# Gated linear attention into a feed-forward layer on one core: blocks of three units become blocks of four, and the second product keeps the weights standing

## The chip, the core and the metric

The kernel runs on one core of a Trainium2 chip. The metric is the device time of one execution in microseconds; each figure for a kernel is a median over runs. TensorE multiplies, VectorE (DVE) and ScalarE (ACT) work elementwise, GpSimd (POOL) does the rest, SyncE (SP) issues the DMAs. Line numbers L... are lines of the kernel before, unless the text says after.

## The reference

Inputs are q, k, v and alpha of shape 4 x 8 x 768 x 48 (batch, heads, sequence, head size) and the weights w_in (384 x 2048) and w_out (2048 x 384). Only what matters:

```python
state = np.zeros((B, H, D, D))
for t in range(S):
    state = alpha[:, :, t, :, None] * state + np.einsum('bhd,bhe->bhde', k[:, :, t], v[:, :, t])
    y[:, :, t] = np.einsum('bhd,bhde->bhe', q[:, :, t], state)
x = y.transpose(0, 2, 1, 3).reshape(B * S, H * D)     # 3072 x 384
h = x @ w_in
g = np.maximum(0.01 * h, h)
out = g @ w_out                                        # 3072 x 384
```

The weights arrive as 64-bit floats, handed over as 64-bit integers, and the kernel turns them into pairs of 32-bit floats itself.

## The kernel before

**Attention.** The 768 positions are cut into 6 chunks of 128. A unit is one chunk of one batch with its 8 heads, so there are 24 units; unit u is chunk u // 4 of batch u % 4. For a unit the kernel builds running products of alpha by scans (`scans`, L282 to L300), scales q and k by them (L308 to L322), multiplies k by q into 128 x 128 scores per head (`scores`, L330), masks these (L333 to L346), turns k (`k_tokens`, L348), and forms y from the scores and the state (`outputs`, L358 to L392) and the new state (`next_state`). y is split into a high and a low part in fp32r (the format in which TensorE reads these floats at a faster rate), which are the input x of the FFN. `attention(first, last)` is a generator that yields between these steps; steps of unit u and u + 1 alternate in it. The first 9 units (`AHEAD`) load q, k and alpha by token, and TensorE transposes them (L258); later units load them in 32 x 4 pieces, four DMAs per tensor (L135), and VectorE turns them by stream transposes (L262).

**FFN.** Three units make a block (`UPB` 3): 384 tokens, 8 blocks. The inner size 2048 is cut into 16 slices f. For each block and slice, `ffn_in` multiplies three weight tiles by x into a 128 x 384 bank in three products each (high by high, high by low, low by high), nine matmuls of 384 columns (L460), ACT and VectorE apply the activation and split the result in `gh` and `gl` (L463 to L472). `ffn_out` (L477 to L489) multiplies it by w_out: the activations of one unit (128 tokens) stand in the array, 384 columns of the weights move, three products for each of three units, nine matmuls (L485). That is 8 x 16 x 18 = 2304 matmuls. A block's sums over f lie in three PSUM banks. `finish` copies each bank by ACT (L495) and writes it out by one DMA of 192 KB (L497), whose rows are 1536 bytes.

**Order.** The weights of a slice f come by six DMAs (L188, L192) and are converted by two ACT and six VectorE operations over 128 x 768 (`converting`, L205 to L243). The tile framework emits instructions in the order of the program, and moves them by its own simulated timeline; `behind` and `issue_after` fix an instruction behind another. The prologue runs the attention of units 0 to 8 and converts slices 0 to 2. Then the slices of blocks 0 and 1 alternate, f by f, with the conversion of the slices ahead of them; the second product follows the first `LAG` 3 items later. From block 2 on the attention of units 9 to 23 runs between the products: each item advances the generator by a set number of steps (`SL`, `LEAD`), some held back behind the `gl` of the last items of blocks 0 and 1 (`HELD`). The line that places them:

```python
items += [(i, f, (SL + (LEAD if i == 2 else 0)) / NF, "b") for i in range(2, NB) for f in range(NF)]
```

The x of a block lies in one of three slots of `large`; `gather` (L409) fills up the last rows by two DMAs. PSUM has two banks `ph` for the first product, three named a and three named b. While blocks 0 and 1 alternate, b holds the sums of block 0 and a those of block 1; later b holds the sums of a block, and a serves the attention.

## Time and profile before

| | |
|---|---|
| median of 3 runs | 540.48 us (540.3 to 542.23) |
| the profiled run | 540.7 us |
| its span, from the first to the last instruction | 539.0 us |
| TensorE busy | 520.6 us, 97% |
| VectorE busy | 380.3 us, 71% |
| ScalarE busy | 234.1 us, 43% |
| mean granted TensorE clock | 0.996 |

The trace is one execution. A window row has a stretch, its length, and for each engine the busy time and, in brackets, the number of instructions. A row of the chain of waits has the start in us, the length, and the engine, the tile and the line that the end of the program goes back to; "DMA" or "issue" in place of an engine is time in which a transfer or nothing visible is waited for; SPq is SyncE's own queue. In the groups a shape such as 128x384 is partitions by elements, and the number ahead of the vertical bar is how many instructions there are.

### The profile page before, as it was taken

The page shows a single profiled execution, that of the slowest core. Times are in us where ns is not written, and L with a number is a line of the kernel's source. Part 1 is how long each engine was busy: PE and PEld are TensorE (multiplying, and loading weights), DVE is VectorE, ACT ScalarE, POOL GpSimd, SP SyncE. Part 2 cuts the span into 40 slices and gives each one's busy share as a digit, 9 for nine tenths or more (in the row PEclk, how much of TensorE's full clock was granted, in tenths as well). Part 3 has the DMA queues.
Part 4 walks back from the last instruction along what each step waited for, and adds up shares of the span by engine and source line. Part 5 has one row for each costly group of instructions (what it writes and reads, how often), then busy time and mean ns, then how long its engine had stood idle before and what let it go on. Part 6 is the DMA issues. An engine that isn't in the chain of part 4 may idle for free.

```text
span 539.0 us, 9954 instructions
## 1 busy us (share of the span) xinstructions
PE 520.6 (97%) x3742; PEld 497.8 (92%) x3742; DVE 380.3 (71%) x694; ACT 234.1 (43%) x494; POOL 64.5 (12%) x140
## 2 busy tenths in 40 slices
PE   6998899999999899999999999999999999999996
PEld 4787789999998799999999999999999999999995
DVE  6899999999999597875685775775876533333331
ACT  2675665545532543435334343344343344233332
POOL 4445420000000022110110101001100000000000
PEclk9998999999999999999999999999999999999999
DMA  9999954545825343433332422413301010101001
GB/s 146 164 177 184 202 140 131 142 111 134 190 43 144 114 107 85 102 79 103 71 82 58 105 64 61 105 42 99 69 1 40 0 45 1 23 0 45 0 1 49
DMA packets 92981, 46.62 MB, mean 86 GB/s; under 512 B 57856, under 2 KB 90112, under 8 KB 92928
## 3 DMA queue, kind: packets, MB, share of 16 engines
q1 hardware_dynamic: 92928, 45.93, 39.4%
q8 instruction: 31, 0.51, 0.4%
q14 instruction: 22, 0.18, 0.1%
HBM read 38.83 MB, written 4.72 MB: 81 GB/s over the span
## 4 chain that ended last, share of the span: by engine, by line
PE 87%; DVE 5%; DMA 3%; issue 1%; SPq 1%; POOL 1%; ACT 1%; DVEq 0%; ACTq 0%; POOLq 0%
PE ph L460 35%; PE b L485 32%; PE a L330 4%; PE a L485 4%; PE a L374 3%; PE a L368 2%; PE b L258 2%; PE a L353 1%; DMA raw<-in_moe_w_in_dram 1%; DMA out_dram<-t 1%; PE a L385 1%; DVE pc L288 1%; PE b L374 1%; PE a L258 1%; DVE rc L294 1%
## 5 line engine op out<-in xcount | busy, mean ns | idle before, releaser
L460 PE MATMUL ph<-large,w 128*128 128x384 f32 x1152 | 225.6, 338 | 3.1 <-DMA raw<-in_moe_w_in_dram 1.9
L460 PEld LDWEIGHTS ph<-large,w 128*128 128x128 f32 x1152 | 200.5, 188 | 5.4 <-DVE t L466 2.2
L485 PE MATMUL b<-w,gh 128*128 128x384 f32 x672 | 169.6, 340 | 1.3 <-ACT t L495 1.3
L466 DVE TENSOR_TENSOR t<-ph,t 128x384 f32<-128x384 f32 x128 | 70.3, 549 | 86.7 <-ACT t L463 86.3
L485 PEld LDWEIGHTS b<-w,gh 128*128 128x128 f32 x672 | 119.5, 188 | 3.7 <-ACT t L495 1.6
L463 ACT ACTIVATE t<-ph 128x384 f32<-128x384 f32 x128 | 62.6, 489 | 136.7 <-PE ph L460 128.6
L468 ACT CAST gh<-t 128x384 fp32r<-128x384 f32 x128 | 65.7, 513 | 108.2 <-DVE t L466 104.7
L485 PE MATMUL b<-w,gl 128*128 128x384 f32 x336 | 107.3, 336 | 0.0
L472 DVE TENSOR_TENSOR gl<-t,gh 128x384 fp32r<-128x384 f32 x128 | 70.3, 550 | 33.6 <-ACT gh L468 30.0
L485 PEld LDWEIGHTS b<-w,gl 128*128 128x128 f32 x336 | 62.6, 188 | 0.1
L341 POOL TENSOR_SCALAR_AFFINE_SELECT sm<-sm 128x512 f32<-128x512 f32 x33 | 21.9, 676 | 117.6 <-ACT sm L340 100.0
L346 POOL TENSOR_TENSOR small<-us,pe 48x192 f32<-48x192 f32 x40 | 25.5, 637 | 85.2 <-DVE us L406 75.3
L330 PEld LDWEIGHTS a<-qs,ks 48*128 48x128 f32 x312 | 26.0, 191 | 6.5 <-issue 5.2
L330 PE MATMUL a<-qs,ks 48*128 48x128 f32 x312 | 31.0, 289 | 0.9 <-DVE ks L321 0.9
L298 POOL COPY pe<-pc 128x4 f32<-128x4 f32 x24 | 5.7, 240 | 175.3 <-DVE pc L288 175.2
L262 DVE STREAM_TRANSPOSE ks<-small 128x512 f32<-128x512 f32 x15 | 16.6, 1119 | 13.6 <-PE a L353 13.6
L340 ACT COPY sm<-a 128x512 f32<-128x512 f32 x24 | 14.0, 584 | 15.1 <-PE b L330 13.3
L288 DVE TENSOR_TENSOR_SCAN pc<-e,small 128x128 f32<-128x128 f32 x60 | 19.9, 391 | 0.0
L485 PE MATMUL a<-w,gh 128*128 128x384 f32 x96 | 19.5, 335 | 0.0
L294 DVE TENSOR_TENSOR_SCAN rc<-e,small 128x511 f32<-128x511 f32 x15 | 19.1, 1272 | 0.2
L374 PE MATMUL a<-sm,small 128*48 128x128 f32 x256 | 18.1, 277 | 1.1 <-POOL sm L341 1.1
L224 ACT ACTIVATE raw<-raw 128x768 f32<-128x768 f32 x16 | 14.6, 915 | 7.0 <-DMA raw<-in_moe_w_in_dram 7.0
(82 smaller groups left out, 542.5 us busy)
## 6 DMA issues: line engine op xcount, KB each, us to landing
raw<-in_moe_w_out_dram SPq DMA_DIRECT2D x16, 384.0 KB, 4.0
small<-in_v_dram SPq DMA_DIRECT2D x24, 192.0 KB, 3.9
raw<-in_moe_w_in_dram SPq DMA_DIRECT2D x32, 144.0 KB, 4.0
out_dram<-t SPq DMA_DIRECT2D x24, 192.0 KB, 2.0
small<-in_alpha_dram SPq DMA_DIRECT2D x32, 96.0 KB, 2.2
small<-in_q_dram SPq DMA_DIRECT2D x30, 96.0 KB, 2.5
small<-in_k_dram SPq DMA_DIRECT2D x30, 96.0 KB, 2.2
small<-in_alpha_dram SPq DMA_DIRECT2D x30, 80.0 KB, 2.4
```

The source lines that it names most:

```text
L288: nc.vector.tensor_tensor_scan(pc[:, p, :], aT[:, p, :], ones.broadcast_to([P, C]), 1.0, ALU.mult, ALU.mult)
L294: nc.vector.tensor_tensor_scan(flat[2][:, NP * C - 2::-1], flat[0][:, NP * C - 1:0:-1], flat[1][:, NP * C - 2::-1], last, ALU.mult, ALU.add)
L330: nc.tensor.matmul(ss[s][:, p, :], ks[lo:lo + D, p, :], qs[lo:lo + D, p, :], start=True, stop=True)
L341: nc.gpsimd.affine_select(out=sm[s], in_=sm[s], compare_op=ALU.is_ge, fill=0.0, base=0, pattern=[[0, NP], [1, C]], channel_multiplier=-1)
L346: nc.gpsimd.tensor_tensor(*scalings.pop(0))
L374: nc.tensor.matmul(y[lo:lo + m, p, :], V[:, c:c + m], masked[u][s][:, p, :], start=not tb and p == 0, stop=p == NP - 1, skip_group_check=True,
L460: nc.tensor.matmul(ph, w_in_of(f, wn, g), xt[:, g, :], start=n == 0, stop=n == 3 * NG - 1)
L463: put(ordered, "ACT", lambda: nc.scalar.mul(t, ph, 0.01))
L466: put(ordered, "DVE", lambda: nc.vector.tensor_tensor(t, ph, t, ALU.max))
L468: put(ordered, "ACT", lambda: nc.scalar.copy(gh, t))
L472: made["gl", i, f] = put(ordered, "DVE", lambda: nc.vector.tensor_tensor(gl, t, gh.bitcast(F32), ALU.subtract))
L485: nc.tensor.matmul(po[j], gt[:, js], w_out_of(f, wn), start=f == 0 and n == 0, stop=f == NF - 1 and n == 2)
```

## The change

- `UPB` goes from 3 to 4 units: 6 blocks of 512 tokens, one chunk of all four batches each. `ffn_in` moves 512 columns in each of its nine matmuls (864 in all), and a bank `ph` is full.
- In blocks 0 to 4 (`TURNED`), `ffn_out` has the weights standing (three tiles of 128 output columns) and 512 columns of activations moving, in the order gh by high, gl by high, gh by low: 9 matmuls of 512 per slice, 720 in all, and three banks hold the sums with output columns as rows. The last block computes as before, with four banks and 12 matmuls of 384 per slice, 192 in all.
- `finish` of a turned block turns each bank by one stream transpose of VectorE (128x512, in 32 x 32 squares; after's line 526) into a tile `o` (three of them) and writes it out by 16 DMAs of 16 KB, 32x4x32 elements in pieces of 128 bytes: 48 DMAs per block (after's line 531).
- `AHEAD` is 8 units; units 10 and 11 too are transposed by TensorE (`on_pe`). `LAG` is 2. Block 0 runs two slices ahead of block 1 (`FORE`). Units 8 to 11 begin in the last slices of blocks 0 and 1, and the rest of them follows behind these; block 2 begins when they are done, and units 12 to 23 run between the products of blocks 2 to 5.
- x has two slots that share the part that is gathered from; the first products and transposes of the program get dummy matmuls beside them (`keep_warm`); the order of the four places of y in its bank turns with the block.

The diff, cut to what is named here and in the prediction:

```diff
--- before.py
+++ after.py
@@ -31,7 +31,7 @@
     NP = H // 2
     NG = DM // P
     NF = DF // P
-    UPB = 3
+    UPB = B
     HB = 64
     BR = HB + D
     GAP = HB - D
@@ -55,11 +55,16 @@
     T4 = 4
     RUN = T4 * D
     PITCH = RUN + GAP
-    AHEAD = 3 * UPB
-    LAG = 3
-    SOON, EARLY = 2, 3
-    LEAD = 8
+    AHEAD = 2 * UPB
+    FORE = 2
+    LAG = 2
+    LEAD, HELD = 9, 10
     SL = 8 * UPB
+    def on_pe(u):
+        return u < AHEAD or u in (AHEAD + 2, AHEAD + 3)
     kinds = ["a", "b"]
@@ -122,7 +127,7 @@
         tb, b = units[u]
         ts = slice(tb * C, (tb + 1) * C)
         t, src = loaded(u, i), (alpha, q, k)[i]
-        if u < AHEAD:
+        if on_pe(u):
             n = H if u or i else H // 2
             for h in range(0, H, n):
                 nc.sync.dma_start(
@@ -334,7 +352,7 @@
         ss = live[u].pop()
         sm = [atp.tile([P, NP, C], F32, name="sm", bufs=3) for _ in (0, 1)]
         for s in (0, 1):
-            if s and u >= AHEAD:
+            if s and not on_pe(u):
                 nc.vector.tensor_tensor(sm[s], ss[s], mask.unsqueeze(1).broadcast_to([P, NP, C]), ALU.mult)
                 continue
             made["sm", u] = nc.scalar.copy(sm[s], ss[s])
@@ -464,52 +483,79 @@
         for step in first:
             next(step, None)
         put(ordered, "DVE", lambda: nc.vector.tensor_tensor(t, ph, t, ALU.max))
-        gh = ffp.tile([P, TB], F32R, name="gh", bufs=LAG + 1)
+        gh, gl = (ffp.tile([P, TB], F32R, name=name, bufs=LAG + 1) for name in ("gh", "gl"))
         put(ordered, "ACT", lambda: nc.scalar.copy(gh, t))
         for step in second:
             next(step, None)
-        gl = ffp.tile([P, TB], F32R, name="gl", bufs=LAG + 1)
         made["gl", i, f] = put(ordered, "DVE", lambda: nc.vector.tensor_tensor(gl, t, gh.bitcast(F32), ALU.subtract))
         return gh, gl
     pos = {}
-    def ffn_out(i, f, gs, tag):
+    TURNED = NB - 1
+    NO = 3
+    def ffn_out(i, f, gs):
         gh, gl = gs
+        turned = i < TURNED
         if f == 0:
-            pos[i] = [bank(tag)[:, 0:DM] for _ in range(UPB)]
-        po = pos[i]
-        for j in range(UPB):
-            js = slice(j * C, (j + 1) * C)
-            for n, (gt, wn) in enumerate(((gh, HIGH), (gh, LOW), (gl, HIGH))):
+            tags = "bbb" if i == 0 else "aaa" if turned else "aaab"
+            pos[i] = [bank(tag)[:, 0:TB if turned else DM] for tag in tags]
+        for j, po in enumerate(pos[i]):
+            js = slice(j * P, (j + 1) * P)
+            for n, (gt, wn) in enumerate(((gh, HIGH), (gl, HIGH), (gh, LOW)) if turned else ((gh, HIGH), (gh, LOW), (gl, HIGH))):
+                w = w_out_of(f, wn)
                 nc.tensor.matmul(
-                    po[j], gt[:, js], w_out_of(f, wn), start=f == 0 and n == 0, stop=f == NF - 1 and n == 2
+                    po, *((w[:, js], gt) if turned else (gt[:, js], w)),
+                    start=f == 0 and n == 0, stop=f == NF - 1 and n == 2,
                 )
         if f == NF - 1:
             finish(i)
     def finish(i):
         for j, po in enumerate(pos.pop(i)):
-            tb, b = units[i * UPB + j]
-            o = ffp.tile([P, DM], F32, name="t")
-            nc.scalar.copy(o, po)
-            r = b * S + tb * C
-            nc.sync.dma_start(out[r:r + P, :], o)
-    items = []
-    for f in range(NF):
-        items += [(0, f, 0, "b"), (1, f, 0, "a")]
-    items += [(i, f, (SL + (LEAD if i == 2 else 0)) / NF, "b") for i in range(2, NB) for f in range(NF)]
-    gs = {}
-    LOADS = [(("v", 4), 0, 0), (("v", 5), 0, 1), (("v", 6), 1, 0), (("v", 7), 1, 1), (("g", 1), 2, None), (("g", 1), 3, None)]
-    STARTS = {62: ("kt", 7), 65: ("kv", 7)}
+            if i == TURNED:
+                tb, b = units[i * UPB + j]
+                o = (ffp.tile([P, TB], F32, name="o", bufs=NO) if j < NO else ffp.tile([P, TB], F32, name="t"))[:, 0:DM]
+                (nc.vector.tensor_copy if j % 2 else nc.scalar.copy)(o, po)
+                nc.sync.dma_start(out[b * S + tb * C:b * S + (tb + 1) * C, :], o)
+                continue
+            t = ffp.tile([P, TB], F32, name="o", bufs=NO)
+            nc.vector.transpose(t, po)
+            for a in range(4):
+                c = j * P + 32 * a
+                for b in range(B):
+                    r = b * S + i * C
+                    nc.sync.dma_start(
+                        out[r:r + C, c:c + 32].rearrange("(m r) c -> r m c", r=32),
+                        t[32 * a:32 * (a + 1)].rearrange("r (b m c) -> r b m c", b=B, c=32)[:, b],
+                    )
+    LOADS = [(("v", 4), 0, 0), (("v", 5), 0, 1), (("v", 6), 1, 0), (("v", 7), 1, 1), (("v", 7), 2, None), (("v", 7), 3, None)]
+    CONVERT = [5, 7]
+    STARTS = {50: ("kv", 5), 62: ("kt", 7)}
+    pending = []
+    def put_in(i, f, steps=None):
+        pending.append((i, f, ffn_in(i, f, steps)))
+    def put_out(n=0):
+        ffn_out(*pending.pop(n))
+    loaded_f = converted = 0
+    def load_next():
+        nonlocal loaded_f
+        if loaded_f < NF:
+            load_weights(loaded_f)
+            loaded_f += 1
     st = attention(0, AHEAD)
-    loaded_f = converted = 0
     for n, _ in enumerate(st):
         if n == 2:
             load_values(NV - 1)
@@ -518,61 +564,79 @@
             with behind(*key):
                 load_weights(f, part)
             loaded_f = f + 1
-        u = AHEAD - EARLY + converted
-        if converted < EARLY and ("ks", u) in made:
-            with behind("ks", u):
+        if CONVERT and ("ks", CONVERT[0]) in made:
+            u = CONVERT.pop(0)
+            with behind("ks", u), behind("sm", u - 1):
                 convert(converted)
             converted += 1
         if n in STARTS:
-            i, f = items[len(gs)][:2]
             with behind(*STARTS[n]):
-                gs[len(gs)] = ffn_in(i, f)
-    kinds[:] = "a"
-    HELD = [(0, 14), (1, 14), (0, 15)] + [(1, 15)] * 5
-    due, emitted = 0.0, 0
-    new = coming = None
-    for n in range(len(items) + LAG):
-        slices = 0
-        if n < len(items):
-            i, f, slices, _ = items[n]
-            if f == 0:
-                if i == 2:
-                    st, held = attention(AHEAD, NU), HELD
-                while i not in ready:
-                    next(st)
-                emitted, due = 0, 0.0
-            if loaded_f < NF:
-                load_weights(loaded_f)
-                loaded_f += 1
-                if loaded_f == NF:
-                    asked, later = later, None
-                    with behind("raw", NF - 1):
-                        for fn, *args in asked:
-                            fn(*args)
-            if n < len(STARTS):
-                pass
-            elif i == 0:
-                if coming is None:
-                    coming = converting(f + SOON, True)
-                    next(coming)
-                old, new, coming = new or iter(()), coming, converting(f + SOON + 1, True)
-                gs[n] = ffn_in(i, f, ((), (coming, new, old, new)))
-            elif i == 1:
-                gs[n] = ffn_in(i, f, ((new, new), (new,)))
-                next(new, None)
-            else:
-                gs[n] = ffn_in(i, f)
-        for half in range(2):
-            due += slices / 2
-            while emitted < due:
-                with behind("gl", *held.pop(0)) if held else nullcontext():
-                    next(st, None)
-                emitted += 1
-            if half == 0 and n >= LAG:
-                i, f, _, tag = items[n - LAG]
-                ffn_out(i, f, gs.pop(n - LAG), tag)
+                put_in(0, len(pending))
+    assert converted == len(pending) == FORE and not LOADS
+    with behind("x", AHEAD - 1):
+        for _ in converting(FORE, True):
+            pass
+    for _ in range(FORE + 1):
+        load_next()
+    st = attention(AHEAD, AHEAD + UPB)
+    new, coming = None, converting(FORE + 1, True)
+    next(coming)
+    put_out()
+    for f in range(NF - FORE):
+        new, coming = coming, converting(f + FORE + 2, True)
+        put_in(1, f, ((), (new, new, coming)))
+        put_out()
+        for _ in range(3):
+            next(new, None)
+        put_in(0, f + FORE, ((), (new,)))
+        next(new, None)
+        if f:
+            put_out()
+        load_next()
+        if loaded_f == NF and later is not None:
+            asked, later = later, None
+            with behind("raw", NF - 1):
+                for fn, *args in asked:
+                    fn(*args)
+        if f >= NF - FORE - 4:
+            with behind("gl", 0, f + FORE):
+                next(st)
+    kinds[:] = "b"
+    put_in(1, NF - 2)
+    put_out()
+    put_out()
+    put_in(1, NF - 1)
+    while pending:
+        for _ in range(8):
+            next(st)
+        put_out()
+    while 2 not in ready:
+        next(st)
+    st, held = attention(AHEAD + UPB, NU), HELD
+    for i in range(2, NB):
+        due, emitted = 0.0, 0
+        while i not in ready:
+            next(st)
+        for f in range(NF):
+            put_in(i, f)
+            for half in range(2):
+                due += (SL + (LEAD if i == 2 else 0)) / NF / 2
+                while emitted < due:
+                    with (behind("gl", i, f - 1) if f else behind("x", (i + 1) * UPB - 1)) if held else nullcontext():
+                        next(st, None)
+                    held = max(held - 1, 0)
+                    emitted += 1
+                if half == 0 and len(pending) > LAG:
+                    put_out()
+    while pending:
+        put_out()
     fine = cst.tile([P, 2 * NU], F32, name="fine")
```

What moves, in the instruction rows of each engine (an operation, its output and inputs by the program's names, its shape, and how often it repeats).

TensorE before, where block 2 begins. `w_1786` is the last slice (15), `w_645`, `w_756` and `w_869` are slices 0, 1 and 2; L460 with `w_645` is the first product of block 2.

```order
L485 MATMUL b<-w_1723,gl 128x384 x3
L460 MATMUL ph<-large,w_1786 128x384 x9
L485 MATMUL a<-w_1723,gh 128x384 x6
L485 MATMUL a<-w_1723,gl 128x384 x3
L460 MATMUL ph<-large,w_645 128x384 x9
L485 MATMUL b<-w_1786,gh 128x384 x6
L485 MATMUL b<-w_1786,gl 128x384 x3
L460 MATMUL ph<-large,w_756 128x384 x9
L485 MATMUL a<-w_1786,gh 128x384 x6
L460 MATMUL ph<-large,w_869 128x384 x9
```

TensorE after, the last rows ahead of block 2 (L479 with `w_571` is its first product). L348 is scores, L371 the turning of k, L388 and L394 y, L405 the new state: the rows are those of units 11 and 12.

```order
L348 MATMUL b<-qs,ks 128x128 x8
L371 MATMUL b<-small,ks 128x112 x4
L388 MATMUL b<-qs,small 112x128 x4
L394 MATMUL b<-sm,small 48x128
L405 MATMUL b<-small,ktok 48x48 x8
L394 MATMUL b<-sm,small 48x128 x7
L348 MATMUL b<-qs,ks 128x128 x8
L371 MATMUL b<-small,ks 128x112 x4
L388 MATMUL b<-qs,small 112x128 x4
L394 MATMUL b<-sm,small 48x128
L405 MATMUL b<-small,ktok 48x48 x8
L479 MATMUL ph<-large,w_571 128x512 x9
```

Before, products of block 2 stand between the last products of blocks 0 and 1, and no attention stands there. After, behind the last second product of block 0 there are 18 products of block 1, and then the attention of units 8 to 11 and the scores, y (in part) and state of unit 12, before the first product of block 2.

SyncE after, in the same place: the outputs of block 0 (L531), the loads of unit 12 (L140), and the gather of block 2 (L435).

```order
L133 DMA small<-in_k_dram 128x8x48 x2
L133 DMA small<-in_alpha_dram 128x8x48
L531 DMA out_dram<-o 32x4x32 x32
L152 DMA small<-in_v_dram 128x8x48
L531 DMA out_dram<-o 32x4x32 x16
L140 DMA small<-in_alpha_dram 32x4x192 x2
L140 DMA small<-in_alpha_dram 32x4x160 x2
L140 DMA small<-in_q_dram 32x4x192 x2
L140 DMA small<-in_q_dram 32x4x160 x2
L140 DMA small<-in_k_dram 32x4x192 x2
L140 DMA small<-in_k_dram 32x4x160 x2
L435 DMA large<-large 16x3x1024 x2
```

SyncE before, where the outputs of blocks 0 and 1 are written (L497).

```order
L497 DMA out_dram<-t 128x384
L135 DMA small<-in_k_dram 32x4x160
L135 DMA small<-in_q_dram 32x4x192 x2
L135 DMA small<-in_q_dram 32x4x160
L497 DMA out_dram<-t 128x384
L135 DMA small<-in_q_dram 32x4x160
L497 DMA out_dram<-t 128x384
```

Before, six outputs stand among loads; after, 48 outputs stand ahead of the loads of unit 12.

VectorE after, behind the last second product of block 0. L526 turns the sums: `b` are block 0's banks, `a` block 1's. L306 holds scans of unit 10, L339 scales k, L356 masks.

```order
L526 STREAM_TRANSPOSE o<-b 128x512
L339 TENSOR_TENSOR ks<-ks,rc 128x512
L526 STREAM_TRANSPOSE o<-b 128x512 x2
L490 TENSOR_TENSOR gl<-t,gh 128x512
L356 TENSOR_TENSOR sm<-b,small 128x512
L426 TENSOR_TENSOR us<-small,b 48x192 x2
L412 TENSOR_TENSOR large<-b,large 112x4x128
L526 STREAM_TRANSPOSE o<-a 128x512
L306 SCALAR_TENSOR_TENSOR pc<-b,small 128x128 x4
```

The fourth turn writes an `o` tile again, and so stands behind the 16 DMAs that read that tile's first content; the scans of unit 10 and everything behind them stand behind the turn.

32 lines of the change are left out of this document (21 added, 11 removed).

## The prediction

> **What bounds the kernel now.** I read the busy times first, then TensorE's windows, then the chain of waits. The page's first lines:
>
> ```profile
> span 539.0 us, 9954 instructions
> ...
> PE 520.6 (97%) x3742; PEld 497.8 (92%) x3742; DVE 380.3 (71%) x694; ACT 234.1 (43%) x494; POOL 64.5 (12%) x140
> ...
> L460 PE MATMUL ph<-large,w 128*128 128x384 f32 x1152 | 225.6, 338 | 3.1 <-DMA raw<-in_moe_w_in_dram 1.9
> L460 PEld LDWEIGHTS ph<-large,w 128*128 128x128 f32 x1152 | 200.5, 188 | 5.4 <-DVE t L466 2.2
> ```
>
> TensorE is busy nearly everywhere, but matmuls overlap in the records (338 ns is the length of one, not its pace). The pace stands in the chain near the end, where nothing else runs:
>
> ```profile
> 496.04 3.12 PE ph L460 x18
> 499.16 3.12 PE b L485 x18
> ```
>
> 3.12 / 18 = 173.3 ns for one product of 384 columns, in the first product (L460) and the second (L485) alike. There are 2304 of them (8 blocks of 288): 399.3 us. What is left of the span is found by counting them in five stretches. The windows of line 460, then of line 485 (columns: stretch, its length, TensorE's and the weight loads' busy time with counts, granted clock, DMA):
>
> ```profile
> 0.00:71.00 71.00, 5.42 (x27) 4.54 (x27) 0.98 1.08 177
> 71.00:164.00 93.00, 52.45 (x263) 46.23 (x264) 1.00 0.51 123
> 164.00:200.00 36.00, 14.56 (x75) 12.39 (x74) 1.00 0.49 127
> 200.00:465.00 265.00, 118.75 (x611) 105.81 (x609) 1.00 0.26 63
> 465.00:539.00 74.00, 34.38 (x180) 31.56 (x180) 1.00 0.05 17
> ```
>
> ```profile
> 0.00:71.00 71.00, 0.00 (x0) 0.00 (x0) 0.98 1.08 177
> 71.00:164.00 93.00, 53.85 (x270) 47.59 (x270) 1.00 0.51 123
> 164.00:200.00 36.00, 13.04 (x63) 10.88 (x63) 1.00 0.49 127
> 200.00:465.00 265.00, 119.93 (x607) 105.70 (x608) 1.00 0.26 63
> 465.00:539.00 74.00, 40.26 (x213) 36.98 (x212) 1.00 0.05 17
> ```
>
> Each stretch less its count times 173.3 ns is the time that TensorE didn't give to the FFN: 66.3 us up to 71, 0.6 up to 164, 12.1 up to 200, 53.9 up to 465, 5.9 at the end. (A matmul on an edge counts twice; that is the 0.9 us by which the parts and 399.3 miss 539.0.) So the kernel is a prologue of 66.9 us, 66 us of attention and its stalls between the products, a tail, and 399.3 us of products at a granted clock of 1.00. The run of this profile took 540.7 us, 1.7 more than the span, and the median of three runs is 540.48. My sum is for that run.
>
> **The products.** Now 6 blocks of 288 or 336: 864 products of 512 columns for the first step, 720 turned ones of 512, and in the last block 192 of 384 columns the old way. The trace has no product of 512 columns. For its bounds I use three rows of the timeline, transposes of 128 columns, each with weights of its own:
>
> ```profile
> 57.23 0.60 PE L258 MATMUL a<-small 128*128 128x128 f32 x4
> 57.67 0.60 PE L258 MATMUL b<-small 128*128 128x128 f32 x4
> 58.10 1.04 PE L368 MATMUL b<-qs,small 112*112 112x128 f32 x8
> ```
>
> Eight start within 0.87 us: 109 ns each, 0.85 ns a column. If a product's column costs half of that, 0.425 ns, then 384 columns are 163.2 ns, and 10.1 of the 173.3 are paid once per product. From this 512 columns take 217.6 + 10.1 = 227.7 ns. The upper bound takes all of the 173.3 as columns: 231.1. The lower takes the 10.1 ns as something that 512 columns hide: 217.6. I take 227.7, since the transposes load weights within 109 ns, so that a load hardly limits at 173; this leaves a cost per product. The sum: 1584 x 0.2277 + 192 x 0.1733 = 394.0 us, 5.3 less than before. Note how little: a third more columns per product, and the same number of columns in all.
>
> The Trainium skill, "TensorE: Matmul & The Clock Gate", section "Back-to-back issue gap", gives N / 2.4 + 2.5 ns: 162.5 ns for 384 columns and 215.8 for 512. The trace disagrees for 384, with 173.3; by the rule for 512 the sum would be 18.9 us below mine, 525.5 us.
>
> **The prologue.** It is set by VectorE's unit pace and then by weights and the mask. Chain rows:
>
> ```profile
> 16.32 1.37 DVE pc L288 x4
> ...
> 36.99 1.37 DVE pc L288 x4
> ...
> 55.39 6.42 DMA raw<-in_moe_w_in_dram
> ...
> 65.50 2.29 POOL small L346
> 67.85 2.30 POOL sm L341 x2
> ...
> 71.36 1.76 PE ph L460 x9
> ```
>
> From unit 2 to unit 6 the scans move by 20.67 us, 5.2 a unit. The change runs 8 units there and not 9, which saves at most 5.2. It saves nothing where the weights (6.4 us of waiting at 55) and the mask are late anyway; weights 1 are still converted before the last unit's x. I take 3 us: 63.9. The dummy matmuls go into time in which TensorE waits.
>
> **Blocks 0 and 1.** All engines, 75 to 160 us:
>
> ```profile
> 75.00:160.00 85.00, 85.00 (x491) 85.00 (x490) 83.67 (x134) 44.49 (x79) 0.00 (x0) 1.00 0.50 120
> ```
>
> VectorE is level with TensorE there (83.67 of 85.00). Groups of VectorE:
>
> ```profile
> L466 DVE TENSOR_TENSOR t<-ph,t 128x384 f32<-128x384 f32 x128 | 70.3, 549 | 86.7 <-ACT t L463 86.3
> ...
> L294 DVE TENSOR_TENSOR_SCAN rc<-e,small 128x511 f32<-128x511 f32 x15 | 19.1, 1272 | 0.2
> L262 DVE STREAM_TRANSPOSE ks<-small 128x512 f32<-128x512 f32 x15 | 16.6, 1119 | 13.6 <-PE a L353 13.6
> ...
> L338 DVE TENSOR_TENSOR sm<-a,small 128x512 f32<-128x512 f32 x15 | 10.3, 690 | 2.9 <-DMA out_dram<-t 2.2 <-PE a L330 0.4
> ...
> L290 DVE RECIPROCAL small<-pc 128x32 f32<-128x32 f32 x24 | 7.7, 321 | 1.4
> ```
>
> Four passes per step of f widen from 549 to 690 ns, 0.56 us, while TensorE's 36 products widen by 36 x 54.4 ns = 1.96. The conversion stays. So TensorE leads, and nothing is added. VectorE's slack gains nothing either: of the stretch up to 164 only 0.6 us are lost now.
>
> **Between block 1 and block 2.** This is the term that decides. Before, 12.1 us are lost from 164 to 200, and the products of block 2 stand in TensorE's row among the last ones of block 1. After, block 2 needs units 8 to 11, all of which come last: the second piece of order in the section on the change shows the end of a long row of attention work with no product in it, which follows 18 products left over from block 1 (4.1 us). I count from the end of block 0's second product, T0. SyncE's queue decides, by the third piece: 48 output DMAs of 16 KB stand ahead of the twelve loads of unit 12, whose scores stand ahead of the first product of block 2. Rows for one issue and one landing:
>
> ```profile
> 133.75 1.95 SPq L135 DMA_DIRECT2D small<-in_alpha_dram  x4
> ...
> 137.70 3.69 SPq L135 DMA_DIRECT2D small<-in_k_dram  x8
> ```
>
> ```profile
> L497 SPq DMA_DIRECT2D out_dram<-t x24: 332/368/1474, 172.0 to 534.8; - x24
> ```
>
> ```profile
> out_dram<-t SPq DMA_DIRECT2D x24, 192.0 KB, 2.0
> ...
> small<-in_k_dram SPq DMA_DIRECT2D x30, 96.0 KB, 2.2
> ...
> large<-large SPq DMA_DIRECT2D x16, 144.0 KB, 4.3
> ```
>
> 5.64 us for twelve loads of 32x4 pieces is 0.47 us each; the old outputs took 0.368. A new output has 128 pieces (32x4) as a load has, so I take 0.47. The path: first turn 1.1 (as a 128x512 stream transpose, 1119 ns), 48 x 0.47 = 22.6, a load of v as one more 0.5, twelve loads 5.6, landing 2.2: T0 + 32.0. Then on VectorE transpose 1.1, reciprocal 0.3, product 0.7, scan 1.3, product 0.7: T0 + 36.1. Then scores, a transposition and the state products of unit 12 on TensorE with copies between them, an estimate of 3: T0 + 39. The other path, four units through three banks, takes between 4 x 5.2 = 20.8 and an estimate of 30 us (a bank is freed later with three than with six), and 4.3 for the two halves of the gather: T0 + 25 to 34, below the first. VectorE's turns of block 1 wait for the DMAs that read the three 'o' tiles, and the scans of units 10 and 11 are queued behind them; that is in the 30. So 39 - 4.1 = 34.9 us, 35, in place of 12.1.
>
> **The blocks behind.** Attention between the products:
>
> ```profile
> 200.00:465.00 265.00, 15.11 (x208) 12.62 (x208) 1.00 0.26 63
> ```
>
> ```profile
> 200.00:465.00 265.00, 265.00 (x1958) 256.74 (x1957) 175.21 (x327) 107.25 (x239) 24.67 (x57) 1.00 0.26 63
> ```
>
> The first row is line 330, the scores, 16 records a unit: 13 units, and about half of a 14th by its other parts; 53.9 / 13.5 = 4.0 us a unit. After, units 13 to 23, 11, lie there: 43.9 us. Turns (three of 1.1 us a block) stand on VectorE, by the second row busy for 175 of 265 us, and outputs of 22.6 us per block on a queue whose loads are fetched two units ahead: I add nothing, and up to 2 us for the range. The tail stays at 5.9, for the last block writes the old way.
>
> **Sum.** 63.9 + 35 + 43.9 + 5.9 + 394.0 = 542.7 us of span, with 1.7 around it 544.4 us, 0.7% over 540.7. 0.5% (2.7 us) is about what a measurement of this kernel can tell from no change: below 537.8 counts as faster, above 543.2 as slower.
>
> **Rivals.**
> (A) The other side: the extra 10.1 ns of a 384-column product is a weight load that 512 columns cover. For it: the load's records are 188 ns, longer than the 173.3 of a product. Against it: the transposes' 109 ns, each with a load. Price: 1584 x 10.1 ns = 16.0 us less, 528.4 us. It decides from 225.4 ns a product on: there the sum equals 540.7 us. The rule of the Trainium skill named above comes out on this side, and the trace, by 173.3 for 384 columns, does not bear it out.
> (B) The output DMAs issue at the old outputs' 0.368 us: 48 x 0.10 = 4.9 us less, then the units' chain (T0 + 34) is as late; 539.5 us. For it: they move 16 KB and not 192. Against it: the issue seems to go by pieces, and they have as many as a load.
> (C) The output DMAs cost more, since 128 bytes in a piece are written and not 768 or 1536. At 1.0 us each the path grows by 25.4 us, 569.8. No row shows a write of 128 bytes. The Trainium skill, "DMA: Bandwidth & Descriptors", section "Specifications", speaks against this change: below 512 B a transfer is a read-modify-write and off line rate; no row here bears it out or denies it.
> (D) Everything in a product goes by columns, 231.1 ns: 5.4 us more, 549.8.
> That the change does not do what it says is no rival: its matmuls and DMAs stand in the order as described.
>
> **How the numbers follow.** Forecast 0.40 (its own range 540 to 549), A 0.30, B 0.12, C 0.06, D 0.12. A is high because a cost that 512 columns hide explains the 188 ns. Range: from A less the prologue's other 2.2 us, 526, to D and the boundaries' 2 us with some of the path's size, 554; it leaves out C and little else. Faster: A, and 0.06 from the low ends of B and the forecast: 0.36. Same: the most of B and the forecast's lower part, 0.17. Slower: 0.47.
>
> **What would show it.** The pace in the last blocks' chain: 227.7 ns x 9 = 2.05 us per group (A: 1.96, D: 2.08). The stretch from the last product of block 0 to the first of block 2: 39 us, with SyncE issuing 48 outputs at 0.47 us before unit 12's loads, and TensorE idle. Full rate from about 74 us on. In blocks 2 to 5, 43.9 us outside the products. A gap under 30 us, or outputs that issue past the loads, would make the term of the transition wrong; a pace under 225 ns would make the sign wrong.

## The result and the profile after

The changed kernel takes 568.62 us (median of 4 runs, 566.87 to 570.37) against 541.27 us for the kernel before (4 runs, 540.3 to 542.23): 1.0505 times as long, with a 95% interval of 1.0461 to 1.055. Slower was the likeliest sign in the forecast, but 568.6 lies above its range (526 to 554). The profiled execution of the changed kernel took 569.6 us, its span 567.9. The page of the changed kernel; the last line is the granted clock in 40 slices:

```profile
span 567.9 us, 9071 instructions
...
PE 525.9 (93%) x3262; PEld 439.5 (77%) x3262; DVE 382.9 (67%) x644; ACT 217.5 (38%) x409; POOL 65.0 (11%) x140
...
PEclk9996879999999999659999999999999999999998
```

TensorE is idle more, and the clock is low in two places, from 43 to 85 us and from 227 to 256 (a slice is 14.2 us long; before, one slice stood at 8 and the others at 9). The chain of waits gives the pace of the new products; the last row is the last second product of block 0:

```profile
196.69 2.04 PE a L509 x9
198.72 2.04 PE ph L479 x9
200.76 2.04 PE b L509 x9
```

2.04 / 9 = 226.7 ns, 1.0 under the forecast's 227.7. The windows of the first product (L479), then of the second (L509):

```profile
0.00:90.00 90.00, 14.30 (x47) 10.01 (x47) 0.89 0.79 144
90.00:203.00 113.00, 59.40 (x243) 45.08 (x241) 1.00 0.39 96
203.00:250.00 47.00, 0.71 (x2) 0.65 (x3) 0.81 0.50 93
250.00:490.00 240.00, 109.75 (x434) 80.62 (x433) 0.99 0.34 68
490.00:568.00 78.00, 35.59 (x144) 26.34 (x142) 0.97 0.11 22
```

```profile
0.00:90.00 90.00, 8.43 (x27) 6.22 (x28) 0.89 0.79 144
90.00:203.00 113.00, 59.89 (x245) 45.82 (x246) 1.00 0.39 96
203.00:250.00 47.00, 4.43 (x18) 2.72 (x16) 0.81 0.50 93
250.00:490.00 240.00, 103.25 (x414) 76.87 (x414) 0.99 0.34 68
490.00:568.00 78.00, 40.69 (x210) 37.34 (x210) 0.97 0.11 22
```

Counted as in the forecast, at 226.7 ns and, for the 192 products of 384 columns in the last row, 173.3 ns (edges counted twice make 1.6 us):

| us | forecast | measured |
|---|---|---|
| prologue, with blocks 0 and 1 | 63.9 | 73.2 + 2.4 = 75.6 |
| between block 1 and block 2 | 35 | 42.5 |
| attention beside blocks 2 to 5 | 43.9 | 47.8 |
| end | 5.9 | 8.0 |
| products | 394.0 | 392.4 |

So 11.7 us of the miss are in the prologue, 7.5 in the transition, 6.0 behind it, and the products are right.

**Prologue.** Waits of the changed kernel: who waited for whom, us in total, times, longest.

```profile
ACT large L411 <- DMA large<-large: 6.3, 1, 6.3
...
PE b L388 <- DVE large L412: 5.8, 1, 5.8
...
PE ph L479 <- DMA large<-large: 4.3, 1, 4.3
```

L411 is the copy of y into x, `large` the tile that holds x. The two slots share the group from which the gather reads. Unit 4 is the first of block 1: its copy writes into that group, and waits until the gather of block 0 has read it. TensorE then has no free bank for the next y. Later TensorE's row stops at the first product of block 1, which waits for the second gather. In the chain:

```profile
39.88 6.04 DMA large<-large
...
71.92 4.68 DMA large<-large
```

**Transition.** SyncE's timeline, then TensorE's (the bracket is the idle time before and what ended it):

```profile
204.04 16.42 SPq L531 DMA_DIRECT2D out_dram<-o  x32
...
221.05 8.70 SPq L531 DMA_DIRECT2D out_dram<-o  x16
229.84 1.81 SPq L140 DMA_DIRECT2D small<-in_alpha_dram  x4
...
236.03 1.23 SPq L435 DMA_DIRECT2D large<-large  x2
```

```profile
229.07 0.99 PE L394 MATMUL b<-sm,small 128*48 128x128 f32 x13
242.34 2.08 PE L348 MATMUL b<-qs,ks 48*128 48x128 f32 x16 [12.28 <-DVE ks L339]
...
249.29 8.09 PE L479 MATMUL ph<-large,w 128*128 128x512 f32 x27 [0.89 <-PE b L405]
```

As forecast, 48 outputs stand ahead of the loads of unit 12. They take 25.1 us (0.52 each), 2.5 more than at 0.47. The attention of units 8 to 11 is done at 230, and TensorE then waits 12.3 us for unit 12's k. Block 2 starts 46.5 us behind the last product of block 0 (200.76 + 2.04 = 202.8), not 39. The granted clock in that stretch is the last but two number, the busy share of the DMA engines the one behind it:

```profile
203.00:230.00 27.00, 26.02 (x282) 22.36 (x280) 17.99 (x37) 12.72 (x30) 7.37 (x16) 1.00 0.24 37
230.00:243.00 13.00, 0.72 (x7) 0.69 (x8) 9.04 (x16) 0.58 (x1) 1.72 (x4) 0.59 0.88 166
243.00:250.00 7.00, 6.11 (x46) 5.30 (x45) 0.70 (x2) 2.35 (x6) 1.61 (x3) 0.50 0.77 174
```

Half the clock from 243 on: the first 27 products take 8.09 us, where 27 x 0.2267 is 6.1. While the 48 outputs are issued, the DMA engines are 24% busy: they are not what holds the queue. The outputs themselves land soon (page, last number):

```profile
out_dram<-o SPq DMA_DIRECT2D x240, 16.0 KB, 1.5
```

### The profile page after: what moved, and what is told of

It reads as the page before. It is cut to its first block, busy times and chain, and to the rows that moved or that the text cites. A ratio compares the mean times of both kernels' runs of the same rounds, so it can differ in the third digit from the quotient of the medians.

```text
span 567.9 us, 9071 instructions
## 1 busy us (share of the span) xinstructions
PE 525.9 (93%) x3262; PEld 439.5 (77%) x3262; DVE 382.9 (67%) x644; ACT 217.5 (38%) x409; POOL 65.0 (11%) x140
## 3 DMA queue, kind: packets, MB, share of 16 engines
q1 hardware_dynamic: 125744, 45.45, 39.5%
## 4 chain that ended last, share of the span: by engine, by line
PE 81%; DVE 8%; DMA 4%; SPq 2%; issue 2%; ACT 1%; POOL 0%; DVEq 0%; ACTq 0%; POOLq 0%
PE ph L479 33%; PE a L509 25%; PE b L509 7%; PE b L394 4%; PE b L348 3%; PE b L388 3%; DMA large<-large 2%; PE b L272 1%; PE ph L165 1%; SPq L531 1%; DVE ks L281 1%; DVE rc L312 1%; PE b L405 1%; DMA small<-in_q_dram 1%; DVE pc L306 1%
## 5 line engine op out<-in xcount | busy, mean ns | idle before, releaser
L479 PE MATMUL ph<-large,w 128*128 128x512 f32 x864 | 219.8, 399 | 8.8 <-DMA large<-large 4.3
L479 PEld LDWEIGHTS ph<-large,w 128*128 128x128 f32 x864 | 162.7, 191 | 44.8 <-issue 5.2
L509 PE MATMUL a<-gh,w 128*128 128x512 f32 x384 | 130.3, 393 | 0.0
L485 DVE TENSOR_TENSOR t<-ph,t 128x512 f32<-128x512 f32 x96 | 65.4, 681 | 93.6 <-ACT t L482 93.5
L482 ACT ACTIVATE t<-ph 128x512 f32<-128x512 f32 x96 | 57.3, 597 | 143.0 <-PE ph L479 140.5
L487 ACT CAST gh<-t 128x512 fp32r<-128x512 f32 x96 | 59.6, 621 | 119.9 <-DVE t L485 117.1
L490 DVE TENSOR_TENSOR gl<-t,gh 128x512 fp32r<-128x512 f32 x96 | 65.8, 685 | 28.0 <-ACT gh L487 19.4
L509 PEld LDWEIGHTS a<-gh,w 128*128 128x128 f32 x384 | 72.0, 188 | 16.0 <-issue 0.6
L509 PE MATMUL a<-gl,w 128*128 128x512 f32 x192 | 75.0, 390 | 0.0
L348 PE MATMUL b<-qs,ks 48*128 48x128 f32 x320 | 31.8, 292 | 12.8 <-DVE ks L339 12.5
L509 PEld LDWEIGHTS a<-gl,w 128*128 128x128 f32 x192 | 36.1, 188 | 7.1
L348 PEld LDWEIGHTS b<-qs,ks 48*128 48x128 f32 x320 | 27.0, 194 | 18.2 <-issue 16.0
L509 PE MATMUL b<-gh,w 128*128 128x512 f32 x96 | 33.7, 404 | 0.0
L394 PE MATMUL b<-sm,small 128*48 128x128 f32 (+1 forms) x368 | 28.6, 279 | 0.2
L388 PE MATMUL b<-qs,small 112*112 112x128 f32 x152 | 21.9, 291 | 6.2 <-DVE large L412 5.8
L388 PEld LDWEIGHTS b<-qs,small 112*112 112x112 f32 x152 | 20.2, 190 | 8.4 <-issue 6.2
L509 PE MATMUL a<-w,gh 128*128 128x384 f32 x96 | 24.3, 338 | 0.0
L394 PEld LDWEIGHTS b<-sm,small 128*48 128x48 f32 (+1 forms) x368 | 20.9, 125 | 4.2 <-POOL sm L359 1.4
```

Source lines behind the costliest of these rows:

```text
L348: nc.tensor.matmul(ss[s][:, p, :], ks[lo:lo + D, p, :], qs[lo:lo + D, p, :], start=True, stop=True)
L388: nc.tensor.matmul(y[0:BR, (p + turn) % NP, :], W[0:BR, p, :], qs[0:BR, p, :], start=p == 0, stop=False, skip_group_check=True)
L394: nc.tensor.matmul(y[lo:lo + m, (p + turn) % NP, :], V[:, c:c + m], masked[u][s][:, p, :], start=not tb and p == 0, stop=p == NP - 1, skip ...
L479: nc.tensor.matmul(ph, w_in_of(f, wn, g), xt[:, g, :], start=n == 0, stop=n == 3 * NG - 1)
L482: put(ordered, "ACT", lambda: nc.scalar.mul(t, ph, 0.01))
L485: put(ordered, "DVE", lambda: nc.vector.tensor_tensor(t, ph, t, ALU.max))
```

## The experiments

Each starts from the changed kernel unless the text says otherwise; ratios are to the kernel before, with 95% intervals. Theory P concerns the prologue, S SyncE's queue, W the clock.

**own_group.**

```diff
-    x_sb, = pieces("large", F32R, (2 * NG + 1, 2, TB))
+    x_sb, = pieces("large", F32R, (2 * (NG + 1), 2, TB))
...
-        at = i % 2 * NG
+        at = i % 2 * (NG + 1)
...
-        turn = i % 2
+        turn = 0
...
-        at, last = i % 2 * (NG + 1), NG
+        at = i % 2 * (NG + 1)
+        last = at + NG
```

> The changed kernel, with a gathered group of its own for each of the two x slots. Theory P (the shared group makes the first x copy of unit 4 wait 6.3 us for the gather of block 0, and TensorE goes cold meanwhile): that wait goes, the first product starts 6 to 9 us sooner, the median falls from 568.6 to 560 to 563 us. Rival P2 (the prologue is late because block 1 needs the last unit of the prologue, whoever shares what): the wait moves elsewhere, the median stays within 2 us of 568.6.

562.85 us, 1.040 (1.0358 to 1.0442): 5.8 us less than 568.6, at the upper end of P's range. The 6.3 us of L411 are gone from the waits, and the first product starts at 46.2 us, not 52.3 (the changed kernel's row, then own_group's):

```profile
52.34 0.73 PE L479 MATMUL ph<-large,w 128*128 128x512 f32 x2
```

```profile
46.19 0.70 PE L480 MATMUL ph<-large,w 128*128 128x512 f32 x2 [1.30 <-DMA large<-large]
```

What is left is the wait for the second gather, with 4.3 us as its longest (the first column is the total over two waits):

```profile
PE ph L480 <- DMA large<-large: 5.6, 2, 4.3
```

P holds, and P2 falls for the larger part.

**gather_by_unit.**

```diff
+                made["g", u] = nc.sync.dma_start(x[lo + D:lo + HB, at:at + NG, n, js], x[lo:lo + D, last, n, js])
...
+                gather(u)
...
-                    gather(u // UPB)
```

> The changed kernel, gathering each unit's x by itself as soon as it is there (four DMAs of 24 KB a unit), the group still shared. Theory P: unit 4 meets only the gather of unit 0, long done, and block 1 waits for one unit's gather and not for four; both waits go (6.3 and about half of 4.3 us) with the cold clock behind the first: 9 to 13 us less, 556 to 560 us. The transition gains up to 2 us more by a shorter gather. Rival P2: within 2 us of 568.6; rival P3 (24 more issues on SyncE's queue cost what the waits cost): 566 to 572.

566.59 us, 1.0472 (1.0439 to 1.0505). The wait of unit 4 goes here too, but the prologue gets back only part of it: SyncE issues four gathers per unit among weights and loads, and the first product of block 1 still waits 4.0 us. P3 is the nearest.

**own_and_swap.** own_group, with the two first products of the loop over slices exchanged for its first turn.

```diff
-        put_in(1, f, ((), (new, new, coming)))
+        first = (1, f) if f else (0, FORE)
+        put_in(*first, ((), (new, new, coming)))
...
-        put_in(0, f + FORE, ((), (new,)))
+        put_in(*((0, f + FORE) if f else (1, 0)), ((), (new,)))
...
+        else:
+            pending.reverse()
```

> own_group, and the first product of slice 2 of block 0 stands ahead of the first product of block 1, which waits for the gather of block 1. Theory P (4.3 us of the lost prologue are TensorE waiting there with other products behind it): 3 to 4.5 us less than own_group, 558 to 560 us. Rival P4 (VectorE's conversion of slice 2 ends no earlier than the gather, so the swapped product waits as long): within 1.5 us of own_group's 562.9.

563.01 us, 1.0408 (1.0384 to 1.0431): no gain; P4. The first products around 70 us:

```profile
68.37 0.73 PE L480 MATMUL ph<-large,w 128*128 128x512 f32 x2 [1.41 <-ACT w L246]
...
71.27 4.18 PE L480 MATMUL ph<-large,w 128*128 128x512 f32 x9 [2.17 <-DMA large<-large]
```

TensorE now waits for the conversion of slice 2 first (ACT w) and then for the rest of the gather, and later for gl and gh.

**before_warm and own_no_dummies**: the dummy matmuls put into the kernel before (the diff), and taken out of own_group.

```diff
+    nc.vector.memset(seed, 0.0)
...
+    keep_warm(6)
...
+                if u == 0 and p % 2:
+                    with tc.issue_after(last.ins):
+                        keep_warm(2)
...
-    nc.gpsimd.memset(seed, 0.0)
```

> The kernel before, with the change's dummy matmuls at the start alone. If the dummies help the first units (clock 0.97 in the first 55 us there): up to 1.5 us less than the kernel before. Rival: no difference, within 1 us, since VectorE and the DMAs set the pace of the first units; or slower by up to 1 us, for the products in front of the first transposes.

545.61 us, 1.0083 (1.0056 to 1.011): slower by 4.8 us, more than any expectation. As in the change, the operand of the dummies is also cleared by VectorE and no longer by GpSimd; what of the 4.8 us is which was not tested.

> own_group without the dummy matmuls in the first units. Theory D (what is left of the prologue's miss is 4.3 us of waiting for the gather of block 1, which the swap could not fill, and up to 4.8 us that the dummies cost as they did in the kernel before): 3 to 5 us less than own_group's 562.9, 558 to 560. Rival D2 (the dummies cost only by the order that they led to in the kernel before): within 1.5 us of own_group. Rival D3 (they help here, since the prologue's products sit on colder clocks): 1 to 3 us more.

565.1 us, 1.0422 (1.0364 to 1.048), which overlaps with own_group's. So the dummies don't explain the prologue's rest here, and D falls; between D2 and D3 the run doesn't decide.

**three_outputs.** One output DMA per bank. This kernel leaves out the right order of the elements inside the rows, so its output is not the reference's; it moves the same bytes with 3 issues per block in place of 48.

```diff
-            for a in range(4):
-                c = j * P + 32 * a
-                for b in range(B):
...
+            nc.sync.dma_start(
+                out.rearrange("(b s) c -> s b c", b=B)[i * C:(i + 1) * C, :, j * P:(j + 1) * P],
+                t.rearrange("r (b c) -> r b c", b=B),
+            )
```

> The changed kernel, with 3 output DMAs of 256 KB per turned block in place of 48 of 16 KB: the same bytes to the same rows, the elements in other places inside them. Theory S (SyncE's queue of 48 issues, 25.8 us, holds back the loads of unit 12 and the gather): the first product of block 2 starts 30 to 35 us behind the end of block 0's last second product and not 46.5; 12 to 16 us less, 553 to 557 us. Rival S2 (the attention of units 8 to 11 through three banks is as late): under 6 us less. Rival S3 (the loads of unit 12 wait for their two buffers anyway): under 6 us less, with the loads seen waiting for unit 10.

560.56 us, 1.0361 (1.0335 to 1.0386): 8.1 us less. Block 2 starts at 235.8 us:

```profile
235.80 6.44 PE L479 MATMUL ph<-large,w 128*128 128x512 f32 x18 [6.97 <-DMA large<-large]
```

That is about 34 us behind block 0, as S gave, but 8.1 and not 12 to 16 us are left at the end of the program. Now the gather alone is waited for, right behind the attention of units 8 to 11: S2 is the next bound and stands close. One thing more differs: unit 12's scores and y, which take 6.95 us ahead of block 2 in the changed kernel, now come behind its first 18 products. So the earlier start is not the queue's alone.

**outputs_on_act.**

```diff
-                    nc.sync.dma_start(
+                    nc.scalar.dma_start(
```

> The changed kernel, with the 48 output DMAs per turned block issued by ScalarE in place of SyncE. Theory S (what costs is standing ahead of the loads and the gather in one queue): these leave at once as with three outputs, 8 us less, unless ScalarE's own copies of scores and x (units 8 to 11) now stand behind 48 issues of 0.45 us, 22 us. I expect both: the loads of unit 12 early, ScalarE's copies late, 562 to 574 us. Rival S4 (the writes themselves hold the DMA engines): no change at all, the loads land as late as before.

581.77 us, 1.0769 (1.0739 to 1.08): worse than either end of what I expected. ScalarE's copies stand behind the issues; one copy of the turned k waits 12.4 us:

```profile
ACT ktok L373 <- DMA out_dram<-o: 15.6, 2, 12.4
```

**late_outputs.**

```diff
-    NO = 3
+    NO = 6
...
-                    nc.sync.dma_start(
+                    put_off.append((
...
+    with behind("g", 2):
+        write_out()
```

> The changed kernel with six 'o' tiles, the same 96 output DMAs of blocks 0 and 1 standing behind the gather of block 2 in SyncE's queue. Theory S (place in the queue is the cost): block 2's first product at 234 to 238 us as in three_outputs and not at 249, the median 559 to 563 us. Rival S5 (moved, not removed: the 96 issues, 45 us, now hold back the loads of units 13 to 16, and block 2 waits for those): block 2 starts early, but its first 80 us take 8 to 12 us more; 566 to 570 us.

569.19 us, 1.052 (1.0496 to 1.0543), the changed kernel's time. Block 2 starts at 238.3 us, 11 earlier, and all of it is paid back: among other things the gather of block 3 comes late in SyncE's queue (issued at 326.1 us and not at 319.8), and it stands in the chain.

```profile
233.47 4.68 DMA large<-large
...
326.70 5.20 DMA large<-large
```

S5's time holds, and its point too: the issues cost wherever they stand in that queue. That block 2 waits for the loads of units 13 to 16, as S5 has it, was not shown.

**turn_on_tensor, turn_first_two, ahead_4, ahead_6.** The outputs turned by TensorE: with own_group for all turned blocks, and without it for blocks 0 and 1 alone.

```diff
-            nc.vector.transpose(t, po)
+            (nc.vector.tensor_copy if j % 2 else nc.scalar.copy)(o, po)
...
+                for j in range(NG):
+                    nc.tensor.transpose(ps[:, j * P:(j + 1) * P], os_[j][:, b * C:(b + 1) * C], ident)
+                (nc.vector.tensor_copy if b % 2 else nc.scalar.copy)(t, ps[:, 0:DM])
+                nc.sync.dma_start(out[r:r + C, :], t)
```

> Own gathered groups, and the turned blocks' outputs turned by TensorE (three copies, twelve transposes of 128x128 per block, four copies, four DMAs of 192 KB) in place of stream transposes and 48 DMAs. Theory P + S: the two savings add, 5.8 + 8.1 us, less 5 x 1.3 us for the transposes at 109 ns: 554 to 561 us. Rival: the transposes and copies stand in the chain of the attention behind block 0 (banks and ScalarE) and take back the 8 us: 562 to 566.

571.64 us, 1.0587 (1.0557 to 1.0617), beyond both the theory and the rival. Block 2 starts at 234.8, 7 us earlier than in own_group, but copies wait for the transposes at each block's end:

```profile
DVE t L536 <- PE b L534: 24.8, 7, 4.3
```

> The changed kernel, with the outputs of blocks 0 and 1 alone turned by TensorE (8 DMAs of 192 KB), and those of blocks 2 to 4 by stream transposes and 48 DMAs as before. Theory T (turn_on_tensor lost its gain in blocks 2 to 4, 43.3 us outside the products in 180 us and not 38.1, 14.0 us in the last stretch and not 8.4, since a block's end waits there for copies and transposes): the start of block 2 as early as in turn_on_tensor, the later stretches as in the changed kernel; 558 to 563 us. Rival T2 (the early start of block 2 is paid back behind it, whatever the later turns): 566 to 572 us.

569.9 us, 1.053 (1.0485 to 1.0574). T falls: block 2 starts at 245.8. The transposes of block 0's output and the attention steps of one unit, in part at half the clock (granted 0.50 from 209 to 215 us), now stand ahead of block 1's last nine products, the last of which starts at 220.4 us and not at 209.4. T2's time is nearer, but not its reason.

ahead_4 and ahead_6 add to turn_on_tensor slices of block 0 ahead of the loop, and spread the attention of units 8 to 11 over the products that are left behind it:

```diff
+    for f in range(FORE, F0):
+        new, coming = coming, converting(f + 2, True)
+        put_in(0, f, ((), (new, new, coming)))
...
+    FORE = F0
```

> As turn_on_tensor, and block 0 runs 4 slices ahead of block 1 in place of 2. Theory F (what is left of the transition is attention with no product beside it, for want of products): two more slices of block 1, 8.2 us, lie beside the attention of units 8 to 11, and the wait for the gather of block 1 (4 us) is hidden by slices 2 and 3 of block 0; against it two slices at VectorE's pace of 6.0 us and not 4.1, 3.8 us: 7 to 9 us less than turn_on_tensor. Rival F2 (VectorE's chain, not TensorE, sets the end of the transition, and products only stretch it): within 3 us of turn_on_tensor.

> As ahead_4 with 6 slices. Theory F: another 8.2 us of products beside the attention, against 3.8 us at VectorE's pace: 11 to 14 us less than turn_on_tensor, 541 to 549 us. Rival F2: within 3 us of turn_on_tensor, or slower by up to 8 us.

575.87 us, 1.0673 (1.0636 to 1.0711), and 585.62 us, 1.0849 (1.0817 to 1.0881). F falls. The windows up to the start of block 2, first and second product, for turn_on_tensor and for ahead_6:

```profile
180.00:234.80 54.80, 8.05 (x34) 5.78 (x32) 0.97 0.46 108
```

```profile
180.00:234.80 54.80, 13.45 (x54) 9.98 (x54) 0.97 0.46 108
```

```profile
180.00:250.00 70.00, 16.24 (x64) 11.76 (x64) 0.93 0.34 81
```

```profile
180.00:250.00 70.00, 22.85 (x89) 15.98 (x87) 0.93 0.34 81
```

54.8 - 88 x 0.2267 = 34.9 us outside the products, and 70 - 153 x 0.2267 = 35.3: 65 more products hid nothing. They were missing before: up to 120 us ahead_6 had done 169 products and turn_on_tensor 234. F2's direction is right, but ahead_6 is 14 us slower and not at most 8. That with three banks each step of a unit waits for the one before, so that products in TensorE's row only lengthen the steps, is my reading and was not tested by itself.

**warm_gap, warm_wait, warm_wait_2, own_and_warm.** Dummies in the 12.3 us.

```diff
+    idle = ps_h.tile([P, 512], F32, name="ph")
+    nc.tensor.matmul(idle[:, 0:C], w_sb[0][0:D, HIGH, 0:P], x_sb[0:D, 1, 1, 3 * C:4 * C], start=True, stop=True)
+    for _ in range(18):
+        nc.tensor.matmul(idle, w_in_of(0, HIGH, 0), xs[1][0][:, 0, :], start=True, stop=True)
```

That is warm_wait_2; warm_gap has 50 of 128 columns without the first line, warm_wait 90 like that first line.

> The changed kernel, with 50 dummy products of 128 columns behind unit 11's attention, in the 12.3 us in which TensorE waits for unit 12. Theory W (what came on top of the forecast's 39 us is a cold clock): the scores of unit 12 take 1.1 us and not 2.1, the first 27 products of block 2 6.1 us and not 8.1; 4 to 6 us less, 563 to 565 us. Rival W2 (the clock matters nothing, since the path goes through SyncE): within 1.5 us of 568.6. Rival W3: the dummies end late and add up to 3 us.

572.96 us, 1.0581 (1.0554 to 1.0608); some of the dummies (16 records) stood inside unit 11's y, and the gather went behind other loads (issued at 243.6). That is W3's way, with 4.3 us and not up to 3. The last dummies ended 3.9 us ahead of unit 12's scores, and these took 2.08 us again, so the run says nothing on W.

> The changed kernel with 90 dummy products that read unit 11's x and so can't start before it is there, ahead of unit 12's scores; every other instruction keeps its place. Theory W (about 5 of the 7.9 us that the transition took over its forecast are the cold clock behind the wait): scores of unit 12 take 1.1 us and not 2.1, the 27 first products of block 2 6.1 us and not 8.1; 3 to 5 us less than the changed kernel's 568.6, unless the dummies outlast the wait. Rival W2 (the path through SyncE alone counts): within 1.5 us.

576.54 us, 1.0668 (1.0619 to 1.0717); the dummies outlasted the wait, and did not raise the clock:

```profile
232.07 17.92 PE L622 MATMUL ph<-large,w 48*128 48x128 f32 x89 [2.90 <-DVE large L412]
```

```profile
231.00:250.00 19.00, 17.93 (x92) 17.93 (x93) 8.05 (x14) 0.00 (x0) 1.72 (x4) 0.57 0.85 188
250.00:256.00 6.00, 6.00 (x48) 5.42 (x48) 0.05 (x1) 2.35 (x6) 0.64 (x1) 0.50 0.29 46
```

> The changed kernel with one dummy product that waits for unit 11's x and 18 of 512 columns and 128 rows behind it, ahead of unit 12's scores; the dummies of warm_wait were 89 of 48 rows, took 17.9 us and outlasted the wait. Theory W: these take 18 x 0.23 to 0.45 = 4 to 8 us, end inside the 12.3 us of waiting, unit 12's scores take 1.1 us and not 2.1, the 27 first products of block 2 6.2 us and not 8.1; 3 to 5 us less than the changed kernel's 568.6. Rival W2 (the path through SyncE alone counts): within 1.5 us.

565.34 us, 1.0447 (1.0407 to 1.0488), 3.3 us less than 568.6; the intervals of the two overlap a little. The trace has what W says; the last row is the window from 242 to 249 us, with a granted clock of 1.00:

```profile
232.03 7.22 PE L623 MATMUL ph<-large,w 128*128 128x512 f32 x18
240.15 1.16 PE L348 MATMUL b<-qs,ks 48*128 48x128 f32 x16 [0.90 <-DVE ks L339]
...
244.51 6.40 PE L479 MATMUL ph<-large,w 128*128 128x512 f32 x27 [0.67 <-issue]
```

```profile
242.00:249.00 7.00, 6.33 (x46) 5.19 (x47) 1.52 (x4) 3.01 (x8) 1.64 (x3) 1.00 0.69 165
```

The scores are the firm sign. The 27 products took 6.4 us in own_and_swap too, without dummies.

> own_group and the dummies of warm_wait_2 together. If the shared group and the cold clock are two separate parts of the miss, their savings add: 568.6 - 5.8 - 3.3 = 559.5, 558 to 561 us. Rival (the clock saves nothing once the prologue is earlier, or the savings overlap): 562 to 564 us.

561.9 us, 1.0374 (1.0348 to 1.0399): 1 us less than own_group, and the intervals overlap. In this profile the dummies missed their aim:

```profile
228.57 4.35 PE L624 MATMUL ph<-large,w 128*128 128x512 f32 x18
236.03 2.08 PE L348 MATMUL b<-qs,ks 48*128 48x128 f32 x16 [3.12 <-DVE ks L339]
```

They began before the clock had fallen, ran at 0.24 us each and were done 3.1 us ahead of the scores. The clock fell in these 3.1 us, and unit 12's scores and y take 2.08 and 1.92 us again (1.16 and 1.13 in warm_wait_2). So the run can't tell whether the two savings add. No version of the changed kernel reaches the kernel before.

## Why the prediction was wrong

- **What bounds, and the products:** right. 226.7 ns against 227.7, 392.4 us against 394.0. The cost per product exists: rivals A (217.6) and D (231.1) are out. From 384 to 512 columns a product grows by 53.4 ns (226.7 - 173.3), 0.417 ns a column, which leaves 13.3 ns per product; the forecast had 0.425 and 10.1, so its assumption of half a transpose's column was close.
- **The prologue is the step that failed:** "I take 3 us: 63.9". It measured 75.6. The step counted a unit less and passed over one line of the change, that the x slots share the gathered group. own_group shows the wait of unit 4 behind it to be 5.8 us. A second wait of 4.3 us stands in the trace: block 1 now holds the last unit of the prologue, so that its gather is on the path; own_and_swap could not fill it, and no run takes it away. The rest, about 1.6 us, is open. The prologue is the largest miss, not the only one: less 11.7 us the time would still be 556.9, above the range.
- **Blocks 0 and 1:** right; only 2.4 us are lost from 90 to 203 us.
- **The transition:** the mechanism and the queue were right, the size was off: 42.5 against 35. Unit 12's scores start 39.5 us behind block 0's last product (242.34 - 202.8), not 36.1: 3.4 us, of which 2.5 are the 48 issues at 0.52 and not 0.47 us. From the scores to block 2 it takes 6.95 us (249.29 - 242.34) where the forecast has "an estimate of 3": 4.0 us more. In warm_wait_2, at the full clock, this takes 4.36 us (244.51 - 240.15), so 2.6 us are the half clock behind the 12.3 us of waiting, which the forecast passed over, and 1.4 the estimate itself. What the clock is worth in the time of the whole program is not settled: warm_wait_2 gained 3.3 us with intervals that overlap.
- **The blocks behind and the end:** 47.8 against 43.9 and 8.0 against 5.9. 2 us of the first are the 27 cold products (8.09 - 6.1); for the rest no run tells.
- **Rivals:** B (0.368 us an issue) is out by 0.52. C gave 569.8, which is nearly the result, by a mechanism that isn't there: an output landed in 1.5 us and issued in 0.52, not 1.0. A matching total proves nothing on its cause.

## What to carry to other kernels

Where a change makes two buffers share a part, look for the first writer of that part and for the slowest reader that it must wait for; here that cost 5.8 us. A stall on TensorE is to be priced with the half-clock work behind it, not with the stall alone. Splitting an output into 16 times as many DMAs cost the queue its issues wherever they stood, and moving them to ScalarE's queue moved the stall to ScalarE's copies.

## What the runs showed of the hardware

- An issue of a 16 KB output of 128-byte pieces took 0.52 us on SyncE in a row of 48 (25.1 us), and landed in 1.5 us at the median (the old 192 KB outputs in 2.0). The Trainium skill, "DMA: Bandwidth & Descriptors", section "Specifications", warns of pieces under 512 bytes, which are read, modified and written, off line rate. With the DMA engines 24% busy beside the 48 issues no price of this shows here, and no run tests for it.
- After 12.3 us without a matmul the granted clock was 0.50. In warm_wait_2 2.8 us without one were enough (0.50 from 232 us on), and in own_and_warm 3.1; 1.4 us in own_and_warm were not. The Trainium skill, "TensorE: Matmul & The Clock Gate", section "What's actually happening", has the clock halved after an idle window of about 3.4 us and freed by a busy one; the idle half agrees in kind, with less than 3.4 us here.
- What frees the clock is only in part shown. 18 products of 128 rows and 512 columns raised it within 7.2 us (0.40 us each on average), and it was 1.00 from 242 to 249 us. 89 products of 48 rows and 128 columns did not in 17.9 us; they took 0.20 us each, and whether their rows, their columns or pauses inside these 0.20 us decide was not tested. In own_and_swap the attention steps of unit 12, products of 48 to 128 rows and at most 128 columns from 238.2 us on, had the clock at 1.00 by 245 us.
